# Second-layer weight copies, load lead and in-place weight sums in a fused attention and two-FFN kernel

## The chip, the cores and the metric

One Trainium2 chip, one core. The metric is the device time of one execution in microseconds; lower is better. The kernel before takes 1645.0 us (median of 3 runs, 1644.35 to 1645.06).

## What is computed

Attention within chunks of 64 tokens, then two feed-forward layers on its output, 4608 tokens of 512 features, 2048 inner features, float32:

```python
scores = scale * q_c @ k_c^T ; attn = softmax(scores) ; x = attn @ v_c     # 8 x 8 heads, 576 = 9 x 64, D = 64
h = x @ w_in ;  g = s * relu(h)**2 + b ;       x = g @ w_out               # first layer (moe)
h = x @ w_in2 ; g = h * sigmoid(1.702 * h) ;   out = g @ w_out2            # second layer (moe2)
```

The weights come in as 8-byte floats (a pair of 32-bit words each), and the kernel decodes them itself.

## The kernel before

**Precision and tiles.** Each matrix product is made of three TensorE passes, on a rounded part (hi) and a remainder (lo) of both operands: lo x hi, hi x hi, hi x lo. Tokens are cut into nine blocks of 512. Weights lie in 16 tiles ("wi" for w_in, "wo" for w_out), each with hi and lo beside each other.

**Plain blocks and pairs.** Of the 18 blocks (nine in each layer) eight are "plain": blocks 0 to 6 of the first layer and block 0 of the second. For each of the 16 weight tiles `gemm_in` does 12 matmuls into an h bank, ScalarE and VectorE make g and its parts, and `gemm_out` does 12 matmuls into four accumulators two steps later. The other ten blocks go in pairs (class `Halves`), each a 2x2 scheme of seven products M1 to M7 instead of eight. For these the weights are needed as seven combinations: three plain quarters and four sums. `PLACE` says where each product's combination lies in DRAM (`wi_sums`, `wo_sums`): places 0 to 2 hold the quarters, places 3 to 6 the sums.

**Time plan.** Everything is entered in a list with `at(t, ...)`; t counts slots, 32 slots to a plain block. The list, sorted by t, gives the priority. In it, an instruction enters its engine's queue when the planner's own estimate says that its operands and rooms are ready; only SP's DMAs before slot 64 are kept in order by hand. Each engine then runs its queue strictly in order. Block z of the first layer (z from 2) begins at slot 32 z; the second layer's plain block is z = 7, slot 224; the pairs begin at slot 260.

**Around the change.**
- `decode_second` (lines 192 to 213, one step each 9.3 slots from slot 56) loads two tiles of second weights into two "wst" rooms (`staged`, three in all), decodes them, stores the decoded tiles to `w2_dram` on GpSimd's DMA queue (L203), makes four sums on GpSimd (`add_quarters`, L221 to L224), rounds them on ScalarE (L209), takes the remainder on VectorE (L211) and stores both to places 3 to 6 (L213).
- `sums` (L234 to L256) does the same for the first weights: hi + lo on VectorE into two "vs" rooms (L240), `add_quarters` into a "wst" room, rounding on ScalarE (L247) into the "vs" rooms, remainder (L252), four stores (L254).
- `copies` (L258 to L263) stores hi and lo of the three plain quarters straight from the resident weights: three DMAs of 256 KB for each tile pair, for either layer.
- `second_weights` (L226 to L229) loads a decoded tile back from `w2_dram` into a "tmp" room (ten in all, also used by relu's r, q, k, p, pt, outputs) with L228, then `resident` splits it into the room that a first weight leaves: ScalarE L150, VectorE L151. The 32 loads run through block 6 of the first layer, from slot 193, wo three slots behind wi.
- `copies(1, ...)` of the second layer start at slots 212 to 229.
- In `Halves`, `load_wi` (L712 to L719) loads the seven combinations in four DMAs of two places each, the last with one, nine slots ahead of use; the products are used in the order M1, M5, M6, M2, M3, M7, M4.

Of the kernel before, what the change touches and what calls it, by code (L numbers as in the profile page):

```python
# [6 lines left out]
F32 = mybir.dt.float32  # L7
F32R = mybir.dt.float32r
I32 = mybir.dt.int32
U32 = mybir.dt.uint32  # L10
AF = mybir.ActivationFunctionType
ALU = mybir.AluOpType
# [4 lines left out]
P = 128  # L17
# [18 lines left out]

PLACE = {"M1": 0, "M2": 1, "M4": 2, "M5": 3, "M6": 4, "M7": 5, "M3": 6}
BANK = {"M1": "x", "M6": "x", "M7": "x", "M4": "x", "M5": "d", "M3": "d", "M2": "b"}  # L40
PAIRS = ((1, 1), (0, 7), (1, 3), (1, 5), (1, 7))
OUT_ORDER = ("M1", "M5", "M6", "M2", "M7", "M3", "M4")
# [3 lines left out]
def chunk_attention_two_ffn(ctx, tc, q, k, v, w1_in, w1_out, s, b, w2_in, w2_out, out):  # L46
# [93 lines left out]
    def staged():  # L140
        return stpool.tile([P, NB_MAX, 2], I32, tag="wst", name="wst")
# [50 lines left out]
    def decode_second(kind, i):  # L192
        tiles = i, i + KF // 2
        sts, ms = [], []
        for t in tiles:
            sts.append(staged())
            load_f64[kind](w2_in if kind == "wi" else w2_out, t, sts[-1])
            yield
        for t, st in zip(tiles, sts):
            m, c = tmp("wm"), tmp("wc")  # L200
            for _ in decode(st, m, c):
                pass
            nc.gpsimd.dma_start(out=w2_dram[kind][t], in_=m)  # L203
            ms.append(m.rearrange("p (t c) -> p t c", c=2 * P))
            yield
        s, hi = (st.rearrange("p f z -> p (f z)").bitcast(F32).rearrange("p (t c) -> p t c", c=2 * P) for st in sts)
        add_quarters(kind, s, ms)
        yield
        nc.scalar.activation(out=hi.bitcast(F32R), in_=s, func=AF.Copy)  # L209
        yield  # L210
        nc.vector.tensor_tensor(out=s.bitcast(F32R), in0=s, in1=hi, op=ALU.subtract)  # L211
        for part, src in enumerate((hi, s)):
            nc.sync.dma_start(out=sums_to(1, kind, i)[:, 3:7, part].rearrange("p m k c -> p m (k c)"), in_=src)  # L213

    def add_quarters(kind, s, tiles):

        one, two = tiles
        a11, a22 = one[:, 0, :], two[:, 1, :]
        a12, a21 = (one[:, 1, :], two[:, 0, :]) if kind == "wi" else (two[:, 0, :], one[:, 1, :])
        s1, s2, s3, s4 = (s[:, t, :] for t in range(4))  # L220
        nc.gpsimd.tensor_tensor(out=s1, in0=a21, in1=a22, op=ALU.add)  # L221
        nc.gpsimd.tensor_tensor(out=s3, in0=a11, in1=a21, op=ALU.subtract)
        nc.gpsimd.tensor_tensor(out=s2, in0=s1, in1=a11, op=ALU.subtract)
        nc.gpsimd.tensor_tensor(out=s4, in0=a12, in1=s2, op=ALU.subtract)  # L224

    def second_weights(kind, i):  # L226
        m = tmp("wm")
        nc.sync.dma_start(out=m, in_=w2_dram[kind][i])  # L228
        W[1, kind, i] = resident(1, kind, i, m)  # L229

    def sums_to(f, kind, i):
        return wi_sums[f][i] if kind == "wi" else wo_sums[f][:, :, i]

    def sums(kind, i):  # L234

        q = []
        for t in (i, i + KF // 2):
            hi, lo = (kept_parts[0, kind, t][:, a, :] for a in range(2))
            q.append(apool.tile([P, NB_MAX], F32, tag="vs", name="vs", bufs=HP))
            nc.vector.tensor_tensor(out=q[-1], in0=hi, in1=lo, op=ALU.add)  # L240
        yield
        q = [t.rearrange("p (t c) -> p t c", c=2 * P) for t in q]
        s = staged().rearrange("p f z -> p (f z)").bitcast(F32).rearrange("p (t c) -> p t c", c=2 * P)
        add_quarters(kind, s, q)
        yield
        for n, hi in enumerate(q):
            nc.scalar.activation(out=hi.bitcast(F32R), in_=s[:, 2 * n:2 * n + 2, :], func=AF.Copy)  # L247
        yield
        to = sums_to(0, kind, i)
        for n, hi in enumerate(q):  # L250
            part = s[:, 2 * n:2 * n + 2, :]
            nc.vector.tensor_tensor(out=part.bitcast(F32R), in0=part, in1=hi, op=ALU.subtract)  # L252
            for a, src in enumerate((hi, part)):
                nc.sync.dma_start(  # L254
                    out=to[:, 3 + 2 * n:5 + 2 * n, a].rearrange("p m k c -> p m (k c)"), in_=src
                )  # L256

    def copies(f, kind, i):  # L258

# [236 lines left out]
    def at(t, f, *a):  # L496
        ITEMS.append((t, len(ITEMS), f, a))
# [461 lines left out]
        plan_attention(j)  # L959
    plan_y(0)  # L960
    for n, (i, kind) in enumerate((i, kind) for i in range(KF // 2) for kind in ("wi", "wo")):
        t = 56 + 9.3 * n
        steps_at([(t + d, 1) for d in (0, 1, 2.5, 4, 6, 8.5, 9.7)], lambda kind=kind, i=i: decode_second(kind, i))
        steps_at([(t + d, 1) for d in (2.2, 2.5, 5, 6.2)], lambda kind=kind, i=i: sums(kind, i))
        at(t + 3, copies, 0, kind, i)
    for i in range(KF):
        for n, kind in enumerate(("wi", "wo")):
            t = NS * (SINGLE - 1) + 2 * i + 1 + 3 * n
            at(t, second_weights, kind, i)
            if i >= KF // 2:  # L970
                at(t + 3, copies, 1, kind, i - KF // 2)
    def first_product(*a):
        G[a] = gemm_in(*a)

# [40 lines left out]
```

## Time and profile before

| | us |
|---|---|
| median of 3 runs | 1645.0 (1644.35 to 1645.06) |
| the profiled execution, its own time | 1644.05 |
| its span, first to last instruction | 1642.3 |
| TensorE matmuls busy | 1584.4 |
| VectorE, ScalarE, GpSimd busy | 1125.5, 823.4, 250.7 |

The profile is one execution recorded by the hardware. Its page gives busy times by engine, the span in slices, the chain of work that ended last and the costliest groups. The trace behind it can be asked for each engine's instructions in order of time, with the idle time ahead of one and what ended it, for waits by engine, and for busy time, granted TensorE clock and DMA share of any stretch.

### The profile page before, as it was taken

The page shows a single profiled execution, that of the slowest core. Times are in us where ns is not written, and L with a number is a line of the kernel's source. Part 1 is how long each engine was busy: PE and PEld are TensorE (multiplying, and loading weights), DVE is VectorE, ACT ScalarE, POOL GpSimd, SP SyncE. Part 2 cuts the span into 40 slices and gives each one's busy share as a digit, 9 for nine tenths or more (in the row PEclk, how much of TensorE's full clock was granted, in tenths as well). Part 3 has the DMA queues.
Part 4 walks back from the last instruction along what each step waited for, and adds up shares of the span by engine and source line. Part 5 has one row for each costly group of instructions (what it writes and reads, how often), then busy time and mean ns, then how long its engine had stood idle before and what let it go on. Part 6 is the DMA issues. An engine that isn't in the chain of part 4 may idle for free.

```text
span 1642.3 us, 24873 instructions
## 1 busy us (share of the span) xinstructions
PE 1584.4 (96%) x8840; PEld 1295.1 (79%) x8840; DVE 1125.5 (69%) x1836; ACT 823.4 (50%) x1427; POOL 250.7 (15%) x286
## 2 busy tenths in 40 slices
PE   6889999999999999999999999999999999999998
PEld 4768887778888888777888788888887888788876
DVE  5667667768776676766745696369368946984685
ACT  3766424445544545545334564776345535543552
POOL 1344214234333334200000000000001000100000
PEclk8899999999999999999999999999999999999999
DMA  9747667666665666899606777786668686777764
GB/s 232 224 159 205 201 171 220 169 178 174 187 170 158 171 193 164 243 278 289 203 27 187 235 224 192 213 274 205 196 193 265 179 225 210 249 192 214 218 194 76
DMA packets 392396, 326.74 MB, mean 199 GB/s; under 512 B 256592, under 2 KB 330320, under 8 KB 392272
## 3 DMA queue, kind: packets, MB, share of 16 engines
q1 hardware_dynamic: 382096, 301.81, 65.0%
q0 software_dynamic: 5760, 18.88, 3.4%
q10 hardware_dynamic: 4416, 4.46, 0.8%
q8 instruction: 70, 1.15, 0.3%
q14 instruction: 54, 0.44, 0.1%
HBM read 232.78 MB, written 92.27 MB: 198 GB/s over the span
## 4 chain that ended last, share of the span: by engine, by line
PE 78%; DVE 7%; DMA 5%; ACT 3%; SPq 2%; issue 2%; POOL 2%; DVEq 0%; POOLq 0%; ACTq 0%
PE acc L629 15%; PE h L554 14%; PE x L735 13%; PE x L834 13%; PE d L834 7%; PE d L735 7%; PE b L735 3%; PE b L834 3%; DMA wm<-w_wi 2%; DVE pt L320 1%; PE xT L330 1%; PE sc L351 1%; SPq L452 1%; SPq L294 1%; DVE gl L103 1%
## 5 line engine op out<-in xcount | busy, mean ns | idle before, releaser
L554 PE MATMUL h<-xh,wi 128*128 128x512 f32 x1024 | 326.1, 400 | 19.1 <-ACT r L566 9.5
L629 PE MATMUL acc<-gh,wo 128*128 128x512 f32 x896 | 277.1, 393 | 2.7 <-ACT gh L102 2.7
L554 PEld LDWEIGHTS h<-xh,wi 128*128 128x128 f32 x1024 | 193.0, 192 | 62.6 <-ACT r L566 11.5
L554 PE MATMUL h<-xl,wi 128*128 128x512 f32 x512 | 202.2, 396 | 0.0
L629 PEld LDWEIGHTS acc<-gh,wo 128*128 128x128 f32 x896 | 166.3, 188 | 38.7 <-ACT gh L102 3.6
L629 PE MATMUL acc<-gl,wo 128*128 128x512 f32 x448 | 172.7, 392 | 2.0 <-DVE gl L103 1.9
L811 ACT ACTIVATE op<-wo 128x512 fp32r<-128x512 f32 x160 | 99.7, 631 | 98.1 <-PE x L834 35.9
L834 PE MATMUL x<-op,wi 128*128 128x512 f32 x540 | 130.7, 389 | 0.0
L735 PE MATMUL x<-xh,wi 128*128 128x512 f32 x400 | 124.3, 391 | 3.1 <-DVE wo L754 3.1
L812 DVE TENSOR_TENSOR op<-wo,op 128x512 fp32r<-128x512 f32 x160 | 107.2, 683 | 17.4 <-ACT op L811 15.9
L834 PEld LDWEIGHTS x<-op,wi 128*128 128x128 f32 x540 | 101.4, 188 | 21.1
L554 PEld LDWEIGHTS h<-xl,wi 128*128 128x128 f32 x512 | 98.3, 192 | 21.1
L659 DVE TENSOR_TENSOR wo<-wo 128x512 f32<-128x512 f32 x160 | 107.4, 686 | 4.5 <-ACT wo L757 3.7
L761 DVE TENSOR_TENSOR wo<-wo,r 128x512 f32<-128x512 f32 x96 | 66.0, 691 | 63.8 <-ACT r L760 63.4
L128 POOL TENSOR_TENSOR wm<-wm,wc 128x512 int32<-128x512 int32 x52 | 73.4, 1414 | 216.0 <-DVE wm L127 111.9
L674 POOL DMA_DIRECT2D xr<-y x32 | 17.6, 549 | 564.5 <-DVE op L812 278.8
L629 PEld LDWEIGHTS acc<-gl,wo 128*128 128x128 f32 x448 | 83.9, 188 | 21.6 <-DVE gl L103 4.0
L320 DVE STREAM_TRANSPOSE pt<-p 32x256 f32<-32x256 f32 x224 | 97.7, 436 | 3.9
L760 ACT ACTIVATE r<-wo 128x512 f32<-128x512 f32 x96 | 60.7, 632 | 75.8 <-DVE wo L754 75.1
L811 ACT ACTIVATE gh<-wo 128x512 fp32r<-128x512 f32 x120 | 74.7, 631 | 47.4 <-PE x L834 13.6
L812 DVE TENSOR_TENSOR gl<-wo,gh 128x512 fp32r<-128x512 f32 x120 | 81.4, 687 | 18.5 <-ACT gh L811 14.3
L735 PEld LDWEIGHTS x<-xh,wi 128*128 128x128 f32 x400 | 74.7, 188 | 20.5 <-DVE wo L754 5.2
(162 smaller groups left out, 3028.6 us busy)
## 6 DMA issues: line engine op xcount, KB each, us to landing
wi<-wo_sums SPq DMA_DIRECT2D x140, 512.0 KB, 4.2
wi<-wi_sums SPq DMA_DIRECT2D x120, 512.0 KB, 4.0
wst<-in_moe_w_out SPq DMA_DIRECT2D x32, 512.0 KB, 4.2
wst<-in_moe_w_in SPq DMA_DIRECT2D x24, 512.0 KB, 4.5
wi_sums<-wi SPq DMA_DIRECT2D x48, 256.0 KB, 4.0
wo_sums<-wo SPq DMA_DIRECT2D x48, 256.0 KB, 4.1
wi<-wi_sums SPq DMA_DIRECT2D x40, 256.0 KB, 3.6
y<-ost SPq DMA_DIRECT2D x36, 256.0 KB, 3.7
```

The costliest lines, as they stand in the source:

```text
L128: nc.gpsimd.tensor_tensor(out=t, in0=t, in1=c.bitcast(I32), op=ALU.add)
L320: nc.vector.transpose(out=pt[r.start + ek * BK:r.start + (ek + 1) * BK, :, eq * BK:(eq + 1) * BK], in_=p[r.start + eq * BK:r.start + (eq + ...
L554: nc.tensor.matmul(out=ps, lhsT=w_[:, kk, :], rhs=x_, start=kk == 0 and a == 0, stop=kk == KD - 1 and a == 2,)
L629: nc.tensor.matmul(out=acc[m], lhsT=l_, rhs=r_, start=i == 0 and a == 0, stop=i == KF - 1 and a == 2)
L659: nc.vector.tensor_tensor(out=to, in0=one, in1=two, op=ALU.subtract)
L674: nc.gpsimd.dma_start(out=t, in_=(y_dram if self.f else x_dram)[self.j + c][:, k + a * HK, :])
L735: nc.tensor.matmul(out=self.ps[key], lhsT=l_, rhs=r_, start=start and k == 0 and a == 0, stop=k == HK - 1 and a == 2, skip_group_check=not ...
L760: nc.scalar.activation(out=r, in_=h, func=AF.Sigmoid, scale=1.702)
L761: nc.vector.tensor_tensor(out=g, in0=h, in1=r, op=ALU.mult)
L811: nc.scalar.activation(out=hi, in_=src, func=AF.Copy)
L812: nc.vector.tensor_tensor(out=lo, in0=src, in1=hi.bitcast(F32), op=ALU.subtract)
L834: nc.tensor.matmul(out=self.ps[key], lhsT=l_, rhs=r_, start=start and i == 0 and a == 0, stop=i == HF - 1 and a == 2, skip_group_check=not ...
```

## The change

1. `second_weights` gets a step between its load and its split; the load is planned three slots ahead of where it was, the split where it was.
2. The second layer's `copies` are planned in the second layer's plain block: slots 226 to 244.5 instead of 212 to 229.
3. `sums` lets `add_quarters` write over its operands in the "vs" rooms, takes the "wst" room only for the rounded values and takes it later (6 instead of 2.5 slots into the step). For "wi" the sums then lie in another order, so `PLACE` changes, and with it the DMA pair in which each combination of `load_wi` comes: M5 moves from the second to the fourth.
4. `decode_second` and `sums` begin at slot 62 instead of 56, and their last parts (rounding, remainder, stores) are planned one slot later within the step.

```diff
-PLACE = {"M1": 0, "M2": 1, "M4": 2, "M5": 3, "M6": 4, "M7": 5, "M3": 6}
+PLACE = {"M1": 0, "M2": 1, "M4": 2, "M6": 3, "M7": 4, "M3": 5, "M5": 6}
...
-        add_quarters(kind, s, ms)
+        add_quarters(kind, ms, [s[:, t, :] for t in (3, 0, 1, 2)])
...
-    def add_quarters(kind, s, tiles):
+    def add_quarters(kind, tiles, to=None):
...
-        s1, s2, s3, s4 = (s[:, t, :] for t in range(4))
+        s1, s2, s3, s4 = to or (a22, a11, a21, a12)
...
         nc.sync.dma_start(out=m, in_=w2_dram[kind][i])
+        yield
         W[1, kind, i] = resident(1, kind, i, m)
...
-        s = staged().rearrange("p f z -> p (f z)").bitcast(F32).rearrange("p (t c) -> p t c", c=2 * P)
-        add_quarters(kind, s, q)
+        add_quarters(kind, q)
         yield
-        for n, hi in enumerate(q):
-            nc.scalar.activation(out=hi.bitcast(F32R), in_=s[:, 2 * n:2 * n + 2, :], func=AF.Copy)
+        his = staged().rearrange("p f z -> p (f z)").bitcast(F32).rearrange("p (t c) -> p t c", c=2 * P)
+        his = [his[:, 2 * n:2 * n + 2, :] for n in range(2)]
+        for src, hi in zip(q, his):
+            nc.scalar.activation(out=hi.bitcast(F32R), in_=src, func=AF.Copy)
         yield
-        to = sums_to(0, kind, i)
-        for n, hi in enumerate(q):
-            part = s[:, 2 * n:2 * n + 2, :]
-            nc.vector.tensor_tensor(out=part.bitcast(F32R), in0=part, in1=hi, op=ALU.subtract)
-            for a, src in enumerate((hi, part)):
-                nc.sync.dma_start(
-                    out=to[:, 3 + 2 * n:5 + 2 * n, a].rearrange("p m k c -> p m (k c)"), in_=src
-                )
+        sums = sums_to(0, kind, i)[:, 3:7]
+        for n, (src, hi) in enumerate(zip(q, his)):
+            nc.vector.tensor_tensor(out=src.bitcast(F32R), in0=src, in1=hi, op=ALU.subtract)
+            to = sums[:, n::2] if kind == "wi" else sums[:, 2 * n:2 * n + 2]
+            for a, part in enumerate((hi, src)):
+                nc.sync.dma_start(out=to[:, :, a].rearrange("p m k c -> p m (k c)"), in_=part)
...
-        t = 56 + 9.3 * n
-        steps_at([(t + d, 1) for d in (0, 1, 2.5, 4, 6, 8.5, 9.7)], lambda kind=kind, i=i: decode_second(kind, i))
-        steps_at([(t + d, 1) for d in (2.2, 2.5, 5, 6.2)], lambda kind=kind, i=i: sums(kind, i))
+        t = 62 + 9.3 * n
+        steps_at([(t + d, 1) for d in (0, 1, 2.5, 4, 6, 9.5, 10.7)], lambda kind=kind, i=i: decode_second(kind, i))
+        steps_at([(t + d, 1) for d in (2.2, 2.5, 6, 7.2)], lambda kind=kind, i=i: sums(kind, i))
         at(t + 3, copies, 0, kind, i)
...
-            at(t, second_weights, kind, i)
+            steps_at(((t - 3, 1), (t, 1)), lambda kind=kind, i=i: second_weights(kind, i))
             if i >= KF // 2:
-                at(t + 3, copies, 1, kind, i - KF // 2)
+                at(NS * SINGLE + 2.5 * (i - KF // 2) + 2 + n, copies, 1, kind, i - KF // 2)
```

## Rows read from the trace of the kernel before

**Rows 1.** The page, busy us (share of the span) and instructions of each engine.
```profile
PE 1584.4 (96%) x8840; PEld 1295.1 (79%) x8840; DVE 1125.5 (69%) x1836; ACT 823.4 (50%) x1427; POOL 250.7 (15%) x286
```

**Rows 2.** Timeline of TensorE: start, us, instruction, in brackets idle us before it, releaser.
```profile
266.61 0.73 PE L554 MATMUL h<-xh,wi 128*128 128x512 f32 x2 [1.99 <-ACT r L566]
291.39 1.22 PE L554 MATMUL h<-xh,wi 128*128 128x512 f32 x2 [4.33 <-ACT r L566]
341.30 0.50 PE L629 MATMUL acc<-gl,wo 128*128 128x512 f32 x1 [1.45 <-DVE gl L103]
393.16 0.73 PE L554 MATMUL h<-xh,wi 128*128 128x512 f32 x2 [0.93 <-ACT r L566]
688.25 0.73 PE L629 MATMUL acc<-gh,wo 128*128 128x512 f32 x2 [2.67 <-ACT gh L102]
727.37 0.50 PE L629 MATMUL acc<-gl,wo 128*128 128x512 f32 x1 [0.43 <-DVE gl L103]
732.19 0.73 PE L554 MATMUL h<-xh,wi 128*128 128x512 f32 x2 [2.26 <-ACT r L566]
769.05 0.44 PE L330 MATMUL xT<-pt,vs 64*64 64x64 f32 x6 [0.65 <-DVE pt L320]
770.96 0.73 PE L554 MATMUL h<-xh,wi 128*128 128x512 f32 x2 [1.47 <-DVE r L570]
```

**Rows 3.** Stretches of 40 us: busy us by engine, granted clock, DMA share, GB/s.
```profile
240.00:280.00 40.00, 38.01 (x264) 30.10 (x263) 29.00 (x44) 16.24 (x28) 15.98 (x18) 0.96 0.80 223
280.00:320.00 40.00, 35.67 (x201) 28.48 (x200) 35.16 (x53) 18.22 (x31) 12.64 (x14) 0.96 0.69 178
```

**Rows 4.** Timeline of ScalarE, splits of second weights; last, a sum of its waits.
```profile
687.04 0.63 ACT L150 ACTIVATE wo<-wm 128x512 fp32r<-128x512 f32 x1 [4.87 <-DMA wm<-w_wo]
721.03 0.63 ACT L150 ACTIVATE wi<-wm 128x512 fp32r<-128x512 f32 x1 [8.44 <-DMA wm<-w_wi]
731.02 0.63 ACT L150 ACTIVATE wo<-wm 128x512 fp32r<-128x512 f32 x1 [2.20 <-DMA wm<-w_wo]
761.29 0.63 ACT L150 ACTIVATE wi<-wm 128x512 fp32r<-128x512 f32 x1 [3.33 <-DMA wm<-w_wi]
769.00 0.63 ACT L150 ACTIVATE wi<-wm 128x512 fp32r<-128x512 f32 x1 [5.03 <-DMA wm<-w_wi]
...
ACT wi L150 <- DMA wm<-w_wi: 30.7, 12, 8.4
```

**Rows 5.** Timeline of SyncE's DMA queue, and one store of GpSimd's.
```profile
686.06 1.10 SPq L263 DMA_DIRECT2D wi_sums<-wi x2
...
696.07 0.41 SPq L228 DMA_DIRECT2D wm<-w_wo  x1
...
716.19 0.34 SPq L228 DMA_DIRECT2D wm<-w_wi  x1
...
690.01 0.56 POOL L203 DMA_DIRECT2D w_wo<-wm  x1 [2.69 <-DVE wm L130]
```

**Rows 6.** Block 6 and the plain block behind it: columns as in rows 3.
```profile
658.00:764.00 106.00, 100.42 (x651) 80.79 (x650) 68.19 (x121) 56.72 (x99) 10.31 (x12) 1.00 0.96 277
764.00:860.00 96.00, 93.88 (x600) 76.87 (x599) 65.77 (x118) 33.79 (x57) 4.41 (x8) 1.00 0.45 137
```

**Rows 7.** Timelines of GpSimd and ScalarE: sums that wait for a room.
```profile
389.83 0.73 POOL L221 TENSOR_TENSOR wst<-vs 128x256 f32<-128x256 f32 x1 [7.62 <-DMA wi_sums<-wst]
...
391.99 0.63 ACT L247 ACTIVATE vs<-wst 128x512 fp32r<-128x512 f32 x1 [4.37 <-POOL wst L223]
...
287.74 1.06 ACT L209 ACTIVATE wst<-wst 128x1024 fp32r<-128x1024 f32 x1 [3.94 <-POOL wst L224]
```

**Rows 8.** VectorE's line 103: ns min/median/max, first and last start; then one instance.
```profile
L103 DVE TENSOR_TENSOR gl<-r,gh x80: 639/685/4230, 273.4 to 763.2; 128x512 fp32r<-128x512 f32 x80
...
278.97 4.23 DVE L103 TENSOR_TENSOR gl<-r,gh 128x512 fp32r<-128x512 f32 x1
```

**Rows 9.** First and last of the nine temporary tiles that are live at 686 us.
```profile
678.87 0.66 ACT L124 ACTIVATE wm<-wst 128x512 f32<-128x512 f32 x1
...
685.05 0.42 SPq L228 DMA_DIRECT2D wm<-w_wo  x1
```

## The prediction

> **What bounds the kernel now.** I read the page first. TensorE is busy for 96% of the span [rows 1], so nothing but its remaining idle time can be won. The next view is TensorE's own timeline, searched for rows that carry idle time ahead of them. Behind the start-up (the first 240 us, which the change hardly touches) and ahead of the paired blocks there are nine such rows, and they fall into two places [rows 2]: four between 266 and 394 us, where block 2 of the first layer begins and the second weights are being decoded (1.99 + 4.33 + 1.45 + 0.93 = 8.70 us), and five between 688 and 771 us, in block 6 and at the change to the second layer (2.67 + 0.43 + 2.26 + 0.65 + 1.47 = 7.48 us). The paired blocks have gaps of their own, which no edit reaches. The two early windows also show a mean granted clock of 0.96 where the others have 1.00 [rows 3]: 0.04 of 40 us is 1.6 us lost twice, 3.2 us, in the matmuls right behind the gaps of 1.99 and 4.33 us; the granted clock falls there from 2.4 to 1.2 GHz and comes back. So the most that this change can give is 8.70 + 7.48 + 3.2 = 19.4 us.
>
> Then I asked who is late. In the second place it is ScalarE every time: it stands in its own order at the split of a second weight (L150), whose operand, loaded by L228, has not landed [rows 4]. The relu, the exponential and the split of g queued behind it are then late, and TensorE waits for these: 687.04 for the gap at 688.25, 721.03 for 727.37, 731.02 for 732.19; the waits at 761.29 and 769.00 hold back the exponential and so VectorE's chain, for 769.05 and 770.96. The loads are late because SyncE's queue is: between the load at 696.07 and the next at 716.19 it issues none, but qs, ks and copies [rows 5]. The 16 DMA engines are full meanwhile, share 0.96 over block 6 against 0.45 over the plain block behind it [rows 6].
>
> **The change, part by part.** Durations are from the profiled execution, 1644.05 us with a span of 1642.3; the median of the runs is 1645.0, 0.95 above it. I subtract from the profiled one and carry the 0.95 over.
>
> *Loads of second weights issued three slots ahead.* A slot is about 3 us (32 slots are 106 us in block 6, 96 us in the plain block) [rows 6], so each of the 32 loads gets some 9 to 10 us more. The waits of ScalarE on them are 4.87, 8.44, 2.20, 3.33 and 5.03 us [rows 4], all shorter. The work is the same: 32 DMAs, 32 splits. Gain: the five gaps, 7.48 us; bounds 0 (the loads are held up elsewhere) and 7.48.
>
> *Copies moved from slots 212 to 229 into 226 to 244.5.* These are 48 DMAs of 256 KB on SP. Moved past on SP's queue: the last second-weight loads, now all at slot 223 or before, and q, k and v loads of the last attention pairs. In the plain block they find a DMA share of 0.45. If all of it left block 6, that would be 12.6 MB, at its 277 GB/s 45 us of transfer time [rows 6]. But I don't count on it: the queue's order is made by readiness in the planner's own estimate, and the pair of copies at 686.06 stands there some 36 us ahead of its slot [rows 5]. Being later in the plan they lose to the loads, and that is what is needed. Gain of its own: none counted. The copies' rooms are wanted again by the paired block's loads, which have nine slots of lead; nothing there becomes late.
>
> *Sums of the first weights taken in place.* Instructions and DMAs are equal in number (two adds, four subtractions or additions on GpSimd, two roundings, two differences, four stores); only the room changes. Before, GpSimd's four need a stage room, of which there are three and the decoding takes two. The row at 389.83 shows the cost: GpSimd waits 7.62 us for a store to land that frees the room, ScalarE's rounding at 391.99 waits 4.37 us for GpSimd [rows 7], and the relu behind it makes the gap of 0.93. The 1.45 at 341.30 has the same shape ahead of it. In place, GpSimd needs no room and the rounding takes one a slot later. Gain 0.93 + 1.45 = 2.38 us, bounds 0 and 2.38.
>
> *Decoding six slots later, its rounding one slot later behind its sums.* The 4.33 us gap follows a rounding at 287.74 that waited 3.94 us for GpSimd [rows 7]; a slot more is 3 us, most of it. A step is two loads and two stores on SP, two stores on GpSimd's queue, five instructions each on ScalarE and VectorE and six on GpSimd; all move together, on GpSimd past the sums alone. But block 2 still begins in the midst of a decoding step, another one. The 6.32 us of gaps at 266 and 291 with the 3.2 us of clock, 9.5 us, can go or come back as they are: bounds 0 and 9.5, and I take the middle, 4.8, as I have no row that is nearer to either end. At the other end two thirds of a step (six of 9.3 slots) enter block 6. The last second weight "wo" 7 is now stored by the plan at slot 204 and loaded at 207, where it was 198 and 210. In the trace that store left at 690.01 [rows 5], about slot 202, four behind its plan; four late again it would leave at 208 and land a slot later. SP then stands at the load for some 2 slots, 6 us, with y, q, k loads behind it, and ScalarE at its split a little. Bounds 0 and the largest gap of this kind, 2.67; I take 2.
>
> *Places.* M5's weights now come in the last of the four loads of a step and are used second. These are issued nine slots ahead, and the last room they wait for is free five slots ahead: 15 us, so nothing.
>
> *Other new waits.* Every queue is put in order anew. For a wait that no row shows I take one gap of the kind seen, 2 us, bounds 0 and 4.33.
>
> Sum: 7.48 + 2.38 + 4.8 - 2 - 2 = 10.7 us less: 1633.4 for the profiled run, 1634 for the median.
>
> **The rivals.**
> (a) *Block 2 keeps its gaps.* The middle term is 0 rather than 4.8: 1639. For it speaks that block 2's start still holds a decoding step.
> (b) *All goes*: 1645 - 19.4 = 1626. Against it speaks that the whole order is new.
> (c) *It does not do what it says.* Copies are issued when ready, as at 686.06, so the DMA engines stay full in block 6; loads need a temporary room and cannot leave sooner. Then the 7.48 stays and 2.38 goes, with as much new: 1643 to 1646.
> (d) *Slower: the temporary rooms run out.* There are ten. At 686 us nine are taken: two operands and two low parts of the decoding, relu's r, a turned p and three second weights [rows 9]. One load a slot, each three slots sooner, makes three more: 12 for 10, as long as the decoding overlaps, which the change lengthens to slot 212, ten steps of block 6. Relu's r then waits for a split that itself waits until TensorE has left the old weight. The four gaps behind relu L566 are 1.99, 4.33, 0.93 and 2.26 [rows 2], 2.4 on average; ten are 24 us, the loads' 7.48 is lost: 1645 - 10.7 + 7.5 + 24 = 1666. It decides from about five such gaps on. Against it: most of the time far fewer than nine are live, r is short, and TensorE has two h banks of slack.
> (e) *GpSimd and VectorE collide more often.* One g difference of 0.69 us in the median took 4.23 us [rows 8], 3.5 more, while GpSimd had both a decoding and a sum in hand. In place, sums no longer wait for a room and may fall beside decoding more often: one of four of the 16 sums would cost 4 x 3.5 = 14 us: 1648.5. Against it: GpSimd's work is the same in sum. The Trainium skill (SBUF — State Buffer, "Who interferes with whom") says that a VectorE instruction with two SBUF inputs and a GpSimd instruction that reads SBUF exclude each other for the whole instruction. By that rule the row at 278.97 is such a collision, and the trace agrees with it: 4.23 beside 0.69 us.
>
> **How the numbers follow.** Chances: the forecast, 1634, 0.45 (its own range 1629 to 1640); (a) 0.18; (b) 0.07; (c) 0.14; (d) 0.11; (e) 0.05. The range runs from 1627 to 1649 and leaves out (b) and (d), 0.18. A measurement of this kernel tells 0.2%, 3.3 us, from no change. Faster by more: the forecast, (a) and (b), 0.70. Within: (c), 0.14. Slower: (d) and (e), 0.16.
>
> **What would show it.** Loads: ScalarE's waits on the wm transfers, 30.7 us for wi alone [rows 4], nearly gone, and no gap between 685 and 772 us. If they are there with rooms as the releaser, (d); with the transfers themselves, (c). Copies: SP's L263 rows of the second layer behind 764 us and a lower DMA share in block 6. Sums: no GpSimd wait on a wi_sums or wo_sums store, and none of the gaps at 341 and 393. Block 2: clock 1.00 from 240 to 320 us, or (a). Gaps at new places of more than 4 us in sum would make the forecast wrong, and so would a wait for tmp rooms ahead of relu.

## The result: 17 us slower, and the profile after

The changed kernel takes 1662.2 us (median of four runs, 1661.2 to 1664.3) against 1645.0: ratio 1.0102, 95% interval 1.0085 to 1.0120. The forecast was 1634. The time lies above its range and on the other side of the kernel before.

The page of the kernel after, busy times of the engines, answers to [rows 1]:

```profile
PE 1590.0 (96%) x8840; PEld 1296.7 (78%) x8840; DVE 1140.8 (69%) x1836; ACT 824.5 (50%) x1427; POOL 255.3 (15%) x286
```

No engine has more to do: the instructions are as many as before. But the same 1836 of VectorE take 15.3 us longer (1125.5 before), and TensorE's 8840 take 5.6 us longer. The span is 1659.6 us, 17.3 more.

TensorE's timeline of the kernel after, rows with idle time ahead of them (start, us, instruction, in brackets idle us and releaser). It answers to [rows 2]:

```profile
266.19 0.73 PE L554 MATMUL h<-xh,wi 128*128 128x512 f32 x2 [1.69 <-ACT r L566]
...
482.01 0.73 PE L629 MATMUL acc<-gh,wo 128*128 128x512 f32 x2 [1.69 <-DVE ost L640]
485.81 0.74 PE L629 MATMUL acc<-gh,wo 128*128 128x512 f32 x2 [2.17 <-DVE ost L640]
601.30 0.68 PE L629 MATMUL acc<-gl,wo 128*128 128x512 f32 x1 [4.04 <-DVE gl L103]
685.55 0.73 PE L629 MATMUL acc<-gh,wo 128*128 128x512 f32 x2 [2.60 <-ACT ost L644]
688.20 1.22 PE L629 MATMUL acc<-gh,wo 128*128 128x512 f32 x2 [1.69 <-DVE ost L640]
729.90 0.73 PE L554 MATMUL h<-xh,wi 128*128 128x512 f32 x2 [1.85 <-ACT r L566]
```

Three places can be told apart. Around 270 and 290 the gaps are other ones but no smaller: 7.2 us in six rows, 6.3 before. Between 400 and 610 the kernel before had none; here there are eight, 11.1 us in sum. Around 690 and 730 they stand as before, 7.0 us for 7.5, but what TensorE waits for is now mostly the outputs of a block (`ost`) and a relu. The gaps at 341 and 393 of [rows 2] are gone.

Stretches of 40 us of the kernel after (busy us by engine, granted TensorE clock, DMA share, GB/s; the first two answer to [rows 3]):

```profile
240.00:280.00 40.00, 35.96 (x259) 27.95 (x258) 23.11 (x36) 13.65 (x23) 6.78 (x7) 1.00 0.50 126
280.00:320.00 40.00, 36.85 (x202) 29.10 (x201) 35.16 (x54) 18.34 (x31) 17.73 (x22) 0.91 0.77 214
480.00:520.00 40.00, 36.14 (x213) 29.34 (x212) 32.32 (x51) 19.45 (x32) 15.39 (x20) 1.00 0.67 190
600.00:640.00 40.00, 38.70 (x272) 31.86 (x273) 29.99 (x44) 14.90 (x26) 19.62 (x23) 0.96 0.54 146
680.00:720.00 40.00, 35.71 (x255) 28.80 (x254) 33.47 (x51) 23.66 (x41) 13.52 (x15) 0.91 0.92 262
720.00:760.00 40.00, 37.26 (x235) 29.39 (x234) 26.67 (x49) 21.30 (x37) 4.51 (x6) 0.96 1.02 279
```

From these stretches the whole difference can be counted. In the thirteen from 240 to 760 us TensorE's idle time (40 less its busy time) is 25.5 us, 14.3 before. The granted clock adds to it: (1 - clock) x busy time is 3.3 + 1.5 + 3.2 + 1.5 us in the four stretches below 1.00, together 9.6, and 2.9 before. So 35.0 us are lost there where 17.2 were: 17.8 more, and the span is 17.3 longer. I use this sum, **the loss from 240 to 760 us**, for every kernel below. It comes from one execution of each and tells nothing of the first 240 us, so differences of a few us in it mean little: lead_copies below has 18.5 us and is faster than the kernel before. The granted clock goes down from 2.4 to 1.2 GHz for a moment behind the gaps at 293 (1.61 us), 601, 685 and 730 us, as it did before behind those at 266 and 291; behind the gap of 2.17 us at 485.81 it stayed up (1.00 in that stretch).

The sums of waits of the kernel after (who waits for whom: us, times, longest):

```profile
ACT wi L150 <- DMA wm<-w_wi: 13.2, 8, 4.0
ACT wo L150 <- DMA wm<-w_wo: 3.4, 5, 1.1
ACT wst L249 <- DMA wi_sums<-wst: 23.7, 7, 5.9
ACT wst L249 <- DMA wo_sums<-wst: 20.3, 6, 4.0
DVE vs L253 <- ACT wst L249: 21.5, 8, 4.5
```

The first two rows are the loads of the second weights: 30.7 us [rows 4] and 11.1 us before. GpSimd's wait for the stores of the stage rooms, 7.62 us in the one row of [rows 7] and 95.6 in sum before, is gone too. Both waits that the change aims at have shrunk, and the kernel is slower. In their place ScalarE now waits 44.0 us for the same stores at its rounding (L249), and VectorE 21.5 us behind that. Before, the same rounding (L247) waited too, 62.6 us, but for GpSimd's four.

### The profile page after: what moved, and what is told of

The parts are those of the page before. It is cut to its first block, busy times and chain, and to the rows that moved or that the text cites. A ratio compares the mean times of both kernels' runs of the same rounds, so it can differ in the third digit from the quotient of the medians.

```text
span 1659.6 us, 24888 instructions
## 1 busy us (share of the span) xinstructions
PE 1590.0 (96%) x8840; PEld 1296.7 (78%) x8840; DVE 1140.8 (69%) x1836; ACT 824.5 (50%) x1427; POOL 255.3 (15%) x286
## 4 chain that ended last, share of the span: by engine, by line
PE 66%; DVE 10%; DMA 8%; POOL 4%; SPq 4%; issue 4%; ACT 3%; DVEq 0%; POOLq 0%; ACTq 0%
PE x L834 13%; PE x L735 13%; PE acc L629 10%; PE h L554 9%; PE d L834 7%; PE d L735 6%; PE b L834 3%; PE b L735 3%; SPq L294 2%; DVE pt L320 2%; DMA wm<-w_wi 1%; DVE gl L103 1%; POOL wm L128 1%; DMA wo_sums<-wst 1%; DMA vs<-in_v 1%
## 5 line engine op out<-in xcount | busy, mean ns | idle before, releaser
L629 PE MATMUL acc<-gh,wo 128*128 128x512 f32 x896 | 281.0, 398 | 9.6 <-DVE ost L640 5.5
L128 POOL TENSOR_TENSOR wm<-wm,wc 128x512 int32<-128x512 int32 x52 | 74.4, 1432 | 252.4 <-DVE wm L127 162.8
L674 POOL DMA_DIRECT2D xr<-y x32 | 17.2, 539 | 542.2 <-DVE op L812 278.9
L812 DVE TENSOR_TENSOR gl<-wo,gh 128x512 fp32r<-128x512 f32 x120 | 81.5, 688 | 18.5 <-ACT gh L811 14.3
```

Source lines behind the costliest of these rows:

```text
L128: nc.gpsimd.tensor_tensor(out=t, in0=t, in1=c.bitcast(I32), op=ALU.add)
L629: nc.tensor.matmul(out=acc[m], lhsT=l_, rhs=r_, start=i == 0 and a == 0, stop=i == KF - 1 and a == 2)
L812: nc.vector.tensor_tensor(out=lo, in0=src, in1=hi.bitcast(F32), op=ALU.subtract)
```

## The experiments

All against runs of the kernel before on the same chip, a different set in each round of experiments; so a ratio is not the quotient of the medians shown here.

| kernel | median us | ratio, 95% interval | VectorE busy us | loss 240-760 us |
|---|---|---|---|---|
| after | 1662.2 | 1.0102 (1.0085-1.0120) | 1140.8 | 35.0 |
| only_lead | 1642.3 | 0.9998 (0.9986-1.0011) | 1128.2 | 21.9 |
| only_copies | 1644.2 | 1.0002 (0.9990-1.0014) | 1127.9 | 19.5 |
| lead_copies | 1641.7 | 0.9981 (0.9970-0.9992) | 1129.2 | 18.5 |
| only_later | 1645.2 | 1.0006 (0.9996-1.0015) | 1126.0 | 19.8 |
| only_inplace | 1656.6 | 1.0073 (1.0056-1.0090) | 1145.9 | 27.2 |
| undo_inplace | 1649.8 | 1.0034 (1.0021-1.0048) | 1124.9 | 22.1 |
| undo_later | 1654.8 | 1.0058 (1.0038-1.0078) | 1145.9 | 28.5 |
| after_tmp11 | 1661.4 | 1.0108 (1.0084-1.0133) | 1142.6 | 34.9 |
| inplace_poolwait | 1658.7 | 1.0083 (1.0057-1.0109) | 1146.5 | 27.7 |
| inplace_vector | 1656.5 | 1.0068 (1.0051-1.0086) | 1150.0 | 27.6 |
| inplace_held | 1643.6 | 1.0000 (0.9988-1.0013) | 1133.5 | 16.1 |
| before_tmp9 | 1651.7 | 1.0039 (1.0026-1.0051) | 1124.5 | 16.7 |
| before_stage4 | 1651.7 | 1.0040 (1.0025-1.0055) | 1129.8 | 22.2 |
| inplace_stage4 | 1661.4 | 1.0103 (1.0081-1.0126) | 1140.0 | 31.6 |
| held_adds | 1655.7 | 1.0071 (1.0048-1.0094) | 1149.8 | 31.4 |
| lead_copies_held | 1643.0 | 1.0002 (0.9992-1.0013) | 1134.9 | 17.9 |
| after_held | 1660.8 | 1.0105 (1.0083-1.0128) | 1137.0 | 34.6 |
| after_short_rem | 1665.1 | 1.0118 (1.0095-1.0140) | 1127.1 | 33.2 |

### Which part costs: one part alone, one part undone

The parts are numbered as in the section on the change. only_lead is the kernel before with part 1 alone (with the step between load and split), only_copies has part 2 alone, lead_copies both, and only_later part 4 alone. only_inplace is the kernel before with part 3 at the old times: the new `sums`, `add_quarters` and `PLACE`. undo_inplace is the changed kernel with the old ones, and undo_later the changed kernel with the times of `decode_second` and `sums` put back.

Expected of only_lead: 

> The kernel before with the loads of second weights three slots sooner, nothing else. Theory R (the stage-room wait that GpSimd bore now stands in ScalarE's and VectorE's order, so the in-place sums cost the time): 4 to 7 us faster than before, 1638 to 1641. Theory T (temporary rooms run out because of the loads' lead): 5 us or more slower than before. Theory P (the shift of the decoding by six slots puts it at worse places against the blocks' ends): as R.

Of only_copies: 

> The kernel before with the second layer's copies planned in the plain block, nothing else. All theories: within 3 us of before; the copies leave the DMA queue nearly when they did, since it takes what is ready.

Of only_later: 

> The kernel before with decoding and sums at slot 62 rather than 56 and their last parts one slot later, nothing else. P: 8 to 17 us slower than before. R and T: within 4 us of before.

Of only_inplace: 

> The kernel before with the sums of first weights in place and the places that go with it, at the old times. R: 8 to 15 us slower than before, with some 40 us of ScalarE waiting for stores out of the stage rooms. T and P: within 3 us of before.

Of undo_inplace: 

> The changed kernel with the sums of first weights as they were (through a stage room taken by GpSimd), the other three edits kept. R: the 12 us that the in-place edit costs alone come back, 1647 to 1652; if lead and copies work together as forecast, 1640. T (temporary rooms, because of the lead): 1658 or more, hardly better than the changed kernel.

Of lead_copies: 

> The kernel before with the loads' lead and the later copies together, nothing else. If the copies' place ahead of the loads was what kept the lead from helping: 4 to 7 us faster than before. If temporary rooms or the DMA engines' load hold it: within 3 us of before, as the lead alone.

Of undo_later: 

> The changed kernel with the decoding and the sums where they were in the plan, no six slots and no slot later: loads' lead, later copies and sums in place. Loads' lead and copies alone gave 1641.7, sums in place alone cost 12: if these add up and the shift costs 5 of the 17 us, 1652 to 1656. If the shift costs nothing beside sums in place, 1659 to 1663.

Measured, as differences of the ratios times 1644.5 us. Sums in place cost 12.0 us added to the kernel before, 12.7 beside lead and copies (1.0058 - 0.9981), 11.2 beside all else (1.0102 - 1.0034). Within their intervals, 3 to 4 us either way, these are one number, and it is two thirds of the loss. The shift costs nothing alone (1.0 us, inside its interval), but 8.7 us beside lead and copies (1.0034 - 0.9981) and 7.2 with sums in place as well (1.0102 - 1.0058). Lead and copies together bring 3.1 us (1.3 to 4.9), each alone nothing; of all the kernels run this is the fastest. Put together in this order: -3.1 + 12.7 + 7.2 = 16.8, which is the whole.

Why the lead brings so little alone is seen in block 6 of only_lead, TensorE:

```profile
689.50 0.50 PE L630 MATMUL acc<-gl,wo 128*128 128x512 f32 x1 [1.72 <-DVE gl L103]
731.99 0.73 PE L555 MATMUL h<-xh,wi 128*128 128x512 f32 x2 [1.24 <-ACT r L567]
738.17 0.79 PE L630 MATMUL acc<-gl,wo 128*128 128x512 f32 x1 [1.83 <-DVE gl L103]
```

The waits on the loads fall there from 41.8 to 17.3 us. What is late next is g's low part, VectorE's, ahead of the first and the last gap; the relu of the middle one still stands behind splits that waited for a load. And the granted clock falls behind the gaps at 689.50 and 738.17: it is 0.96 in both stretches from 680 to 760 us, where it was 1.00 before.

### Is it the temporary rooms?

after_tmp11, the changed kernel with eleven temporary rooms instead of ten; the running total of wo, which was a tile of its own, takes the eleventh for as long as it lives:

```diff
-tpool", bufs=10
+tpool", bufs=11
-    wo_total = const.tile([P, NB_MAX], F32, name="wo_total")
...
+            wo_total = tmp("wo_total")
```

> The changed kernel with an eleventh temporary room (it is the one that the running total of first-layer weights held for the whole time; that total now takes a temporary room until it is used). T: 8 us or more faster than the changed kernel, 1654 or less. R: within 4 us of the changed kernel, 1658 to 1666.

Measured: 1.0108, and a loss of 34.9 us, the same as without. So the lack of a temporary room, rival (d), is not the cause.

### What of the sums in place costs: the four's early start?

One place of the trace suggests a mechanism. First the kernel before: the difference behind the gap at 341.30 [rows 2], and what GpSimd does beside it:

```profile
339.49 1.76 DVE L103 TENSOR_TENSOR gl<-r,gh 128x512 fp32r<-128x512 f32 x1
339.20 1.50 POOL L128 TENSOR_TENSOR wm<-wm,wc 128x512 int32<-128x512 int32 x1 [5.52 <-DVE wm L127]
```

Then the same place in only_inplace, VectorE's rows, GpSimd's, and the gap of TensorE:

```profile
339.13 1.21 DVE L103 TENSOR_TENSOR gl<-r,gh 128x512 fp32r<-128x512 f32 x1
340.27 1.51 DVE L127 TENSOR_SCALAR wm<-wm 128x512 int32<-128x512 int32 x1
341.69 1.22 DVE L130 SCALAR_TENSOR_TENSOR wm<-wst,wm 128x512 int32<-128x512 int32 x1
342.84 1.75 DVE L103 TENSOR_TENSOR gl<-r,gh 128x512 fp32r<-128x512 f32 x1
...
345.66 2.05 DVE L103 TENSOR_TENSOR gl<-r,gh 128x512 fp32r<-128x512 f32 x1
...
338.95 0.84 POOL L221 TENSOR_TENSOR vs<-vs 128x256 f32<-128x256 f32 x1 [12.97 <-DVE vs L240]
339.76 1.73 POOL L128 TENSOR_TENSOR wm<-wm,wc 128x512 int32<-128x512 int32 x1
341.45 0.92 POOL L222 TENSOR_TENSOR vs<-vs 128x256 f32<-128x256 f32 x1
342.33 1.71 POOL L128 TENSOR_TENSOR wm<-wm,wc 128x512 int32<-128x512 int32 x1
...
340.40 0.50 PE L628 MATMUL acc<-gl,wo 128*128 128x512 f32 x1 [3.28 <-DVE gl L103]
```

In place, GpSimd's four need no stage room. They start right behind VectorE's additions and alternate with the decoding's L128, and VectorE's instructions beside them take 1.2 to 2.1 us instead of 0.4 to 0.7. These rows show the stretching, not what it costs. The difference that TensorE waits for here took 1.21 us, less than the 1.76 before, and ended 0.9 us earlier; TensorE waits 3.28 us instead of 1.45 because it got here 2.7 us sooner. And no gap follows the stretched instructions behind it until 395 us. This gives **theory V**, so far only suggested: VectorE loses time beside the early four, in front of g's low parts. The rival, **theory S**: ScalarE's rounding now waits for the stores itself, and holds relu, the exponential and the outputs back. The expectations of the earlier runs set nearly the same two against each other, as collisions of GpSimd's four with VectorE (theory C, where a letter stands; theory V is wider and counts all time that VectorE loses there) and as the wait of the rounding for its room (theory R).

inplace_poolwait, only_inplace with a one-column GpSimd write into the stage room, meant to make the four wait for it as before:

```diff
+        his = staged()...
+        nc.gpsimd.memset(his[:, 0:4, 0:1], 0.0)
         add_quarters(kind, q)
```

> The kernel before with sums in place, and one more instruction: GpSimd writes one column of the stage room ahead of its four, so that the room is taken, and waited for, in GpSimd's order instead of ScalarE's. R: at most 4 us slower than before (the 12 us of the in-place edit alone go by two thirds or more), ScalarE's waits on stores at the rounding gone. If the cost lies in the longer hold of the vs rooms or in GpSimd beside VectorE: still 8 us or more slower than before.

Measured: 1.0083. It did not do what was meant: the planner let the four run ahead of the write, and the rounding still waited, now behind the write. So both causes stayed in. But it tells something of theory S, once the next kernel stands beside it. inplace_held is the same with the order forced:

```diff
+        for ins in nc.cur_bb.bb.instructions[old:]:
+            if ins.engine == mybir.EngineType.Pool:
+                tc.add_manual_dep(ins, first.name, IN_ORDER, reason="behind the room")
```

> Before with sums in place, GpSimd's four held behind a one-column write of GpSimd to the stage room, so that they wait for that room as before. In the run with that write alone, the four did not wait for it and ran ahead of it. C and R: within 4 us of before, stretch near 48 us. If it is the vs rooms' longer hold or the other order of places: still 8 us or more slower.

Measured: 1.0000, as both theories forecast. All 12 us are back, with the sums still in place and the new places. The waits for it, first in inplace_poolwait, then in inplace_held:

```profile
ACT wst L249 <- POOL wst L244: 47.8, 14, 5.7
```

```profile
ACT wst L254 <- POOL vs L222: 27.4, 7, 4.4
ACT wst L254 <- POOL vs L223: 26.8, 7, 7.1
ACT wst L254 <- POOL vs L224: 6.9, 10, 1.8
POOL wst L244 <- DMA wi_sums<-wst: 61.5, 8, 9.3
POOL wst L244 <- DMA wo_sums<-wst: 42.7, 6, 9.5
```

ScalarE's rounding waits longer in the faster kernel (61.1 us) than in the slower one (47.8), so the sum of these waits is not what costs. That does not clear theory S, since what counts is what stands behind a wait. In only_inplace, ScalarE and TensorE:

```profile
591.73 1.15 ACT L248 ACTIVATE wst<-vs 128x512 fp32r<-128x512 f32 x2 [5.57 <-DMA wo_sums<-wst]
593.42 0.73 PE L553 MATMUL h<-xh,wi 128*128 128x512 f32 x2 [1.06 <-ACT r L565]
...
676.97 1.15 ACT L248 ACTIVATE wst<-vs 128x512 fp32r<-128x512 f32 x2 [3.06 <-DVE wi L151]
678.83 0.73 PE L628 MATMUL acc<-gh,wo 128*128 128x512 f32 x2 [2.58 <-ACT ost L643]
...
395.81 0.50 PE L628 MATMUL acc<-gl,wo 128*128 128x512 f32 x1 [1.30 <-DVE gl L103]
```

The relu and the output that TensorE waits for at 593.42 and 678.83 stand right behind a rounding that waited; the gap at 395.81 goes back, over VectorE's remainder and transposes, to a rounding that waited 2.07 us for a store. (The VectorE instruction named at 676.97 had ended 1 us before; at the same place of undo_later, ahead of a gap of 3.34 us, the rounding waits 5.58 us for a store.) That is 4.9 us in three gaps. inplace_poolwait has the same three (1.67, 1.12 and 1.58 us), inplace_held none of them. So holding the four takes away both at once, their early start and these gaps behind the rounding, and the two runs don't tell V from S. GpSimd waits 104.2 us for stores again, and that costs nothing. VectorE is busy 8.0 us longer there than in the kernel before (1133.5), and that costs nothing either.

inplace_vector puts the four of `sums` on VectorE:

```diff
-        add_quarters(kind, q)
+        add_quarters(kind, q, on=nc.vector)
```

> Before with sums in place, their four additions and subtractions on VectorE instead of GpSimd (64 instructions, some 0.4 us each, 25 us more on VectorE). Theory C (in place, GpSimd begins these four right behind VectorE's two adds and so works beside VectorE, whose instructions stretch: 69 us of stretch rather than 48, and those on TensorE's path come late): within 4 us of before, stretch near 48 us or less. Theory R (ScalarE's wait for the stage room): still 8 us or more slower than before.

Measured: 1.0068. The forecast of theory R came out, that of theory C did not. The four no longer run beside VectorE, but they are VectorE's own, 64 instructions, and its time is higher still (1150.0), which theory V, the wider one, allows; and the gap behind a rounding that waited for a store is there too (1.49 us at 399.09). By itself this can't tell V from S.

before_stage4 and its control before_tmp9, nothing in place. The fourth stage room needs space, so both have nine temporary rooms, and the running total among them:

```diff
-tpool", bufs=10
+tpool", bufs=9
-stpool", bufs=3
+stpool", bufs=4
```

Expected of before_stage4: 

> The kernel before, nothing in place, with a fourth stage room (in the place of one temporary room and of the running total, which takes a temporary room until it is used), so that GpSimd's sums need not wait for a room. C: 6 to 12 us slower than the same with three stage rooms, stretch 60 us or more, though nothing is in place. R: no slower, or faster, since no engine waits for that room.

Of before_tmp9: 

> Control for the fourth stage room: the kernel before with three stage rooms and the temporary rooms of that one (nine, with the running total in one until it is used). All theories: within 5 us of before.

Measured: both 1651.7. The loss of the control up to 760 us is that of the kernel before (16.7); its 7 us are lost behind that, with fewer rooms as its only edit. With the fourth room GpSimd's wait for stores falls from 95.9 to 30.2 us, and the time stays: the forecast of the collisions, 6 to 12 us, did not come. But the pair settles less than that. In the profiled executions the loss from 240 to 760 us is 5.5 us larger with the fourth room (22.2 for 16.7) and VectorE's time 5.3 us; that the second layer still starts at the same time (764.6 us, 764.7 in the control) goes with a higher granted clock in the first 240 us (0.98, 0.96 in the control), which this edit does not aim at.

### Is it VectorE's time?

held_adds, inplace_held with each of VectorE's two additions done twice, 32 more instructions and no other change:

```diff
-            nc.vector.tensor_tensor(out=q[-1], in0=hi, in1=lo, op=ALU.add)
+            for _ in range(2):
+                nc.vector.tensor_tensor(out=q[-1], in0=hi, in1=lo, op=ALU.add)
```

> The kernel with sums in place and GpSimd's four held behind the stage room (1643.6 us), in which VectorE does each of the two additions hi + lo of a first weight twice: 32 more instructions of some 0.6 us, 20 us of VectorE time at the place where the early four made VectorE late, and no other change. Theory V (time that VectorE loses there is what costs): slower than the kernel before by 8 us or more, 1653 to 1660. Theory S (ScalarE's waits for stores): nothing lost, 1641 to 1647, since VectorE is busy for only 69% of the span. Between 1647 and 1653: VectorE's time costs a part.

Measured: 1.0071. VectorE's time rises from 1133.5 to 1149.8 us, by 16.3, and the time by 12, as theory V forecast. VectorE is busy for 69% of the span, and yet this added work costs three quarters of itself. Its gaps lie at several places: 2.00 us behind an output (379.47), 1.04 behind a relu (418.92), 2.02 and 1.06 behind g's low parts (442.97, 640.88), and those behind late loads around 700 and 740 grew from 5.0 to 8.7 us. So time that VectorE loses in these steps can cost this much. It does not show that the early four cost it in this way.

inplace_stage4, only_inplace with four stage rooms (and nine temporary ones):

> Sums in place alone, with four stage rooms instead of three and nine temporary rooms beside the running total as in the control before_tmp9 (1651.7 us, whose loss lies in the paired blocks). A rounding should hardly wait for a store (34 us in the kernel with in-place sums alone). Theory S: the 12 us go with the waits, the first layer ends within 4 us of before's and the time is 1650 to 1655. Theory V: the four still run beside VectorE, the second layer's plain block begins 8 us or more later than before's, and the time is 1659 to 1666.

```profile
ACT wst L251 <- DMA wo_sums<-wst: 15.4, 6, 4.6
ACT wst L251 <- DMA wi_sums<-wst: 10.8, 4, 3.0
```

Measured: 1.0103; against its control (1.0039) sums in place cost 10.5 us again. The stores' waits fell only from 34.5 us to 26.2, less than meant. Only one gap, 0.91 us at 540.35, goes back to a rounding that waited for a store. So this speaks against theory S as the whole cause, but weakly.

### Does it hold in the whole change?

lead_copies_held has lead, copies and sums in place with the four held; after_held is the whole change with the four held.

> The loads' lead, the later copies and the sums in place with the four held, without the shift by six slots. Loads' lead and copies alone gave 1641.7. If holding makes the in-place sums free, 1639 to 1644, at or below the kernel before; if the three disturb each other as in the whole change, 1648 or more.

> The whole change, with GpSimd's four held behind a one-column write to the stage room. If the early four cost here what they cost alone, 1645 to 1651, close to the whole change without its in-place sums (1649.8), and VectorE's busy time falls from 1140.8 to 1127 to 1134 us. If the whole change loses its 17 us for another reason, 1656 or more.

Measured: 1.0002 and 1.0105. Without the shift holding takes away 9.2 us of 12.7 (undo_later 1.0058); 3.5 us stay (1.0002 - 0.9981). With the shift it takes away nothing, though the four do wait:

```profile
POOL wst L245 <- DMA wi_sums<-wst: 52.1, 7, 10.3
POOL wst L245 <- DMA wo_sums<-wst: 46.6, 6, 9.3
```

after_short_rem is the changed kernel in which VectorE takes the 32 remainders of `sums` over 64 of 512 columns only:

```diff
-            nc.vector.tensor_tensor(out=src.bitcast(F32R), in0=src, in1=hi, op=ALU.subtract)
+            nc.vector.tensor_tensor(out=src[:, :, 0:32].bitcast(F32R), in0=src[:, :, 0:32], in1=hi[:, :, 0:32], op=ALU.subtract)
```

> The changed kernel, in which the 32 remainders of the first weights' sums on VectorE are taken over 64 of 512 columns only; the rest of the low parts is left unsubtracted, so the low parts of the sums are not what they should be. Everything else, stores too, is as in the changed kernel. VectorE's time should fall by 32 x 0.6 = 19 us, from 1140.8 to some 1122. Theory V (VectorE's lost time is the cause in the whole change too): 1651 or less, and TensorE's idle time and lost clock from 240 to 760 us fall from 35 us to 25 or less. If the order of the work or the waits is the cause: 1657 to 1664.

```profile
L253 DVE TENSOR_TENSOR vs<-vs,wst 128x64 fp32r<-128x64 f32 x32 | 8.7, 283 | 25.1 <-ACT wst L249 24.3 <-POOL vs L223 0.6
```

Measured: 1.0118. VectorE works 13.7 us less than in the changed kernel, and neither the time nor the loss (33.2 us) moves; most of TensorE's gaps stand at the same places. So in the whole change VectorE's amount of work is not the cause; theory V in its plain form falls there. (The stretching is hardly touched by this: 79 of VectorE's instructions are stretched beside GpSimd, as counted in the last section, 77 in the changed kernel.) What the shift brings can be seen where block 4 ends. ScalarE and VectorE in the kernel after, then the gaps there of undo_inplace and of after_held:

```profile
589.71 1.15 ACT L249 ACTIVATE wst<-vs 128x512 fp32r<-128x512 f32 x2 [4.34 <-DMA wi_sums<-wst]
590.76 0.62 ACT L364 ACTIVATE p<-p 128x512 f32<-128x512 f32 x1
...
593.47 3.58 DVE L320 STREAM_TRANSPOSE pt<-p 32x256 f32<-32x256 f32 x8
597.08 0.69 DVE L241 TENSOR_TENSOR vs<-wi 128x512 f32<-128x512 f32 x1
597.69 0.42 DVE L127 TENSOR_SCALAR wm<-wm 128x512 int32<-128x512 int32 x1
598.02 0.68 DVE L241 TENSOR_TENSOR vs<-wi 128x512 f32<-128x512 f32 x1
598.63 1.49 DVE L127 TENSOR_SCALAR wm<-wm 128x512 int32<-128x512 int32 x1
600.04 1.21 DVE L103 TENSOR_TENSOR gl<-r,gh 128x512 fp32r<-128x512 f32 x1
```

```profile
593.73 0.50 PE L630 MATMUL acc<-gl,wo 128*128 128x512 f32 x1 [3.22 <-DVE gl L103]
```

```profile
597.57 0.80 PE L635 MATMUL acc<-gl,wo 128*128 128x512 f32 x1 [3.70 <-DVE gl L103]
```

With the shift a step of decoding and of sums begins just where the attention's transposes are queued. In the kernel after, the exponential starts at 590.76, behind a rounding that waited 4.34 us for a store; its operand was ready at 587.5. Then eight transposes, two additions and two parts of the decoding stand ahead of one g difference, and TensorE waits for it: 4.04 us in the kernel after, 3.22 with the old sums, 3.70 with the four held. In the kernel before the place had no gap. A remainder that is shorter doesn't help there, as none stands in this queue. But this place is not the shift's price by itself: only_later has a gap of 2.49 us there (590.00 us) and takes no longer than the kernel before.

**What stays open.** Where sums in place stand alone, holding the four brings the 12 us back, but whether the four beside VectorE cost them or the rounding's wait for its room is not separated: no run has the four early and the rounding without its wait. In the whole change holding brings nothing, so there the cause of the 11 us is not shown: after_held and undo_inplace both have their four wait for the stage room and are 11.7 us apart (idle 24.1 and 17.6 us, lost clock 10.5 and 4.5 from 240 to 760 us, mostly at the same places). And where the shift's 7 to 9 us beside other edits arise is not shown either: undo_inplace loses 3.6 us more than lead_copies from 240 to 760 us, and their times differ by 8.7.

## Why the prediction was wrong

*Loads issued three slots ahead, -7.48.* The first half was right: ScalarE's waits on the transfers fell from 41.8 to 16.6 us, and they did not lack a room, as rival (c) had it. The second half failed: that the gaps go with the waits. There are 7.0 us now, mostly behind outputs and a relu, and the granted clock is 0.91 and 0.96 where it was 1.00. Alone the edit gave 0.9998, and with the copies 3.1 us. I gave the gap to the wait that ended last, without asking how far behind it the next one was; in only_lead that was VectorE's low part of g, for gaps of 1.72 and 1.83 us.

*Sums in place, -2.38.* This is the step that failed by most: +12 us alone, +11 beside the rest. GpSimd's wait for these stores went, as forecast. The two gaps did not go with it: in only_inplace they are 3.28 us (340.40) and 1.30 us (395.81), and neither undo_inplace nor only_later, both with the old sums, has one there, so in the changed kernel it was the shift that moved them. The gap of 1.45 us at 341.30 was misread, too: the difference ahead of it took 1.76 us beside the decoding's L128 instead of 0.69, and no room changes that. Above all I priced the wait as a loss alone. What its end would bring was put at nothing in the sum: that ScalarE's rounding would wait for the rooms itself (34.5 us alone, 44.0 in the changed kernel), with relu, exponential and outputs behind it, and that the four would run beside VectorE (busy 20.4 us longer alone). Held, both go, and so do the 12 us alone (inplace_held); which of the two costs them is open, and in the changed kernel holding brings nothing (after_held). The step asked who waits for GpSimd, and not who would wait in its place or whom it disturbs while it does not wait.

*Block 2, -4.8, a middle between 0 and 9.5.* The gaps there with the clock are 7.2 + 3.3 = 10.5 us, 9.5 before: rival (a), with nothing gained. The shift's price at other places, 7 to 9 us beside the other edits, was in no term: I looked for what it leaves in block 2 and what it brings into block 6, and not at the boundaries between, where its steps fall anew. Against the 2 us that I put for other new waits stand eight new gaps of 11.1 us between 400 and 610 us, which the prediction itself named as a sign of being wrong.

*Copies, places, the w_wo store.* No gain for the copies alone was right (1.0002). They moved little, as rival (c) had it: 36 of the 48 leave before the second layer's first activation, 41 before, and the DMA share just ahead of it (720 to 760 us) is 1.02, 1.03 before. The places cost nothing (inplace_held has them). No run shows the 2 us for the later w_wo steps by themselves; ScalarE's waits on the wo loads fell from 11.1 to 3.4 us.

*The rivals.* (d) ended on the right side with nearly the right time, 1666, by luck: its mechanism is one that after_tmp11 excludes. (e) named one of the two candidates for the in-place part: GpSimd beside VectorE, four cases at 3.5 us, 14 us. Measured are 12 us and a VectorE that works 20.4 us longer in only_inplace, made of many small losses (0.4 to 0.7 us becoming 1.2 to 2.1) rather than of four large ones. I gave it 0.05 on the ground that GpSimd's work is the same in sum; the sum was the same, the overlap was not.

## What to carry to other kernels

Taking away a wait of an engine off the path moves two things: the freed work starts at another moment, beside other work on the neighbour engine, and whatever still needs the room waits for it in another engine's order. Look at both before pricing the wait as a gain. The waits that an edit aims at are no measure of its gain; ask of each gap how far behind its releaser the next late operand is. A sum of waits doesn't tell what they cost either: here the faster kernel had the larger one. And where a step is moved by a fixed number of slots, look at every boundary that one of its repeats now falls on, not at the first and the last.

## What the runs showed of the hardware

VectorE's instructions take longer beside GpSimd, by kind. An instruction counts as stretched where it takes over 0.25 us more than the median of its form. In the kernel before 59 of its 1836 are, 48 us in sum; in only_inplace 88, 69 us, about as much more as its busy time rose, 20.4 us. Every one of them overlaps a GpSimd instruction. All have two inputs or are of the form TENSOR_SCALAR, as L127 (0.42 us in the median, up to 1.57); of the 53 transposes and 17 reductions (L359, L366) that overlap a computing GpSimd instruction in the kernel before none is stretched. The Trainium skill (SBUF — State Buffer, "Who interferes with whom") states that the two engines share a pair of ports, for which VectorE's instructions with two inputs in SBUF and its two-port modes contend with GpSimd, while a reduction doesn't contend. The trace agrees: L127 took 1.51 us beside GpSimd's L128 in only_inplace, 0.42 in the median, and no reduction was stretched.
